# Paced loads, a query-major first group, warm-up matmuls and a reordered end in a grouped-query attention kernel

## The chip, the cores and the metric

The kernel runs on one core of a Trainium2 chip. The metric is the device time of one execution in microseconds. A core has four engines that matter here: PE (matmuls, and weight loads shown as PEld), ACT (activations, here exponentials), DVE (vector operations) and POOL (copies). A fifth, SP, issues all DMAs of this kernel, one after the other in the order of the program. Engines run on their own and are tied by semaphores.

## The reference

Attention with 32 query heads that share 8 key and value heads, batch 16, 288 queries, 512 keys, head size 128, all bfloat16:

```
B, Hq, Hkv, Sq, Sk, D = 16, 32, 8, 288, 512, 128
k = jnp.repeat(k, Hq // Hkv, axis=1)
v = jnp.repeat(v, Hq // Hkv, axis=1)
scores = jnp.einsum("bhqd,bhkd->bhqk", q, k) * D ** -0.5
p = softmax(scores, axis=-1)
out = jnp.einsum("bhqk,bhkd->bhqd", p, v)
```

## The kernel before

**Groups and chunks.** The four query heads of one key head are handled together: 4 x 288 = 1152 query rows, NT = 9 tiles of 128, against 512 keys, NJ = 4 tiles of 128. There are NG = 16 x 8 = 128 such groups. The 4 x 1152 score columns of a group are worked in NC = 3 chunks of CH = 1536 columns, so there are NS = 384 chunks, numbered n. In an ordinary group the columns are key-major: chunk 0 has all 1152 queries of the first key tile and some of the second. The last group (LASTG = 127) is query-major: each chunk has three query tiles against all four key tiles (`pieces`, line 479).

**Steps of a chunk.** `op_s` (line 490, matmul at 499) writes scores S(n) into one of two PSUM buffers ps_s; with two buffers, S(n) waits for the exponential of n - 2. `op_exp` (529, activation at 541) makes the exponential E(n) into pt_sb. The maximum isn't subtracted; at the end the kernel looks at all row sums, and a branch leads to a general path (line 17) if one lies outside a wide range. `op_pv` (509, matmul at 522) makes batch PV(r) of three query tiles from the four key tiles of pt_sb and of the values, with a column of ones added to the values, so that the row sums come out beside the results. It waits for all three exponentials of its group. DVE then takes the reciprocal of the sums (`op_rc`, 556) and scales the batch into o_sb (`op_ev`, 561), which has NO = 6 groups; a scaling waits until the store of the group six before has landed. PV(r) waits for the scaling of r - 2, because ps_o has two banks.

**Order.** PE's order is a loop (line 630): S(n), then PV(n - LAG), LAG = 4. POOL copies each group's values beside the ones (`op_vc`, 544). ACT runs the exponentials in order.

**SP's order.** Queries and keys are loaded with transposing DMAs (`op_q` 448, `op_k` 425), values with plain ones (`op_v` 437). The list `first` (601) loads keys, queries and values of groups 0 to 3 one by one. After it SP branches to its main part and issues a list sorted by a written-out index, in chunks (605 to 617): units of four groups of keys and values (three slots, NSLOT), one q load per group (twelve slots, NQ), one store per group. An index only sets the order; an item also waits for what it needs: a load for its slot, a store for its group's scalings. Loads whose slot has never been used have negative indices, and so stand at the front.

**The end.** The last batch, PV(383), goes to a score buffer instead of ps_o. DVE takes its three reciprocals at once and scales two tiles; ACT scales the third (`op_ev_last`, 574). DVE then looks at the last sums (`op_over`, 590), PE adds the counts over partitions (637), DVE writes a flag (682), every engine loads it and branches. The last group is stored in three parts (472).

Of the kernel before, what the change touches and what calls it, by code (L numbers as in the profile page):

```python
# [6 lines left out]
ACTF = mybir.ActivationFunctionType  # L7
AX = mybir.AxisListType
BF16 = mybir.dt.bfloat16
# [278 lines left out]
def bass_standalone__gqa_softmax__near_ridge_kernel(  # L288
# [6 lines left out]
    B, Hq, Sq, D = q.shape  # L295
    _, Hkv, Sk, _ = k.shape
    P = 128
# [17 lines left out]
    NSLOT = 3  # L315
    NQ = 12
    NPT = 3
    NO = 6
    NS = NG * NC
    LASTG = NG - 1  # L320
# [8 lines left out]
    with ExitStack() as es:  # L329
# [7 lines left out]
        flag_i = es.enter_context(nc.sbuf_tensor("flag_i", [1, 1], I32))  # L337
        block = es.enter_context(nc.Block())

        for name in ["s_go", "s_one", "s_s", "s_e", "s_pv", "s_rc", "s_ev", "s_stat", "s_bad", "s_flag", "s_vc", "s_ol", "s_ea"]:  # L340
            S(name)
        for i in range(NSLOT):
            S("us_k%d" % i)
# [5 lines left out]
            S("s_q%d" % i)  # L349
        for i in range(NO):  # L350
            S("s_o%d" % i)


        gen = ExitStack()
# [4 lines left out]
        def general(eng, key, after):  # L359

            home[key] = nc.cur_bb
            eng.br(after + key)
            with nc.body("general_" + key):
                if key == "sp":
                    eng.sem_inc(sem["s_go"], 1)
                fns[key](eng)
                eng.br("done_" + key)
            nc.switch_bb(after + key)
# [27 lines left out]
        ck_sb = main.enter_context(nc.sbuf_tensor("ck_sb", [P, 3], FP32))  # L396
        bad_sb = main.enter_context(nc.sbuf_tensor("bad_sb", [P, 2, ALONE + 1], FP32))
        one_f = main.enter_context(nc.sbuf_tensor("one_f", [P, 1], FP32))
        dum = main.enter_context(nc.sbuf_tensor("dum", [P, 2], FP32))
        ps_s = main.enter_context(nc.psum_tensor("ps_s", [P, 2, CH], FP32))  # L400
        ps_o = main.enter_context(nc.psum_tensor("ps_o", [P, 2, BANK], FP32))
# [46 lines left out]
        def op_q(g):  # L448
# [3 lines left out]
                    eng.wait_ge(s, n)  # L452
            eng.dma_start_transpose(qt_sb[:, g % NQ], q_v[g * P:(g + 1) * P]).then_inc(sem["s_q%d" % (g % NQ)], 16)  # L453

        def have(kind, g):

            u = g // UG
            if u == 0:
                return ("s_%s%d" % (kind, g), 16)
            return ("us_%s%d" % (kind, u % NSLOT), 16 * (u // NSLOT + (0 if u % NSLOT == 0 else 1)))  # L460

        def op_store(g, i=None):
            eng = nc.sync
            if i is None:
                for (s, n) in need(eng, [("s_ev", NC * (g + 1))]):
                    eng.wait_ge(s, n)
                eng.dma_start(o_v[g], o_sb[:, g % NO].rearrange("p t d -> p (t d)")).then_inc(sem["s_o%d" % (g % NO)], 16)
            else:
                for (s, n) in need(eng, [("s_ev", NC * g + i + 1)] + ([("s_ea", 1)] if i == NC - 1 else [])):
                    eng.wait_ge(s, n)  # L470
                c0, c1 = i * TPC * D, (i + 1) * TPC * D
                eng.dma_start(o_v[g][:, c0:c1], o_sb[:, g % NO].rearrange("p t d -> p (t d)")[:, c0:c1]
                              ).then_inc(sem["s_ol"], 16)
# [4 lines left out]

        def pieces(g, i):

            if g == LASTG:
                w = TPC * P
                cuts = sorted(set(range(0, CH + 1, BANK)) | set(range(0, CH + 1, w)))
                return [(a, a // w, i * w + a % w, b - a) for a, b in zip(cuts[:-1], cuts[1:])]
            lo, hi = i * CH, (i + 1) * CH
            cuts = sorted({lo, hi} | {x for x in range(0, COLS, BANK) if lo < x < hi}
                          | {x for x in range(0, COLS, R) if lo < x < hi})
            return [(a - lo, a // R, a % R, b - a) for a, b in zip(cuts[:-1], cuts[1:])]

        def op_s(n):  # L490
            eng = nc.tensor
            g, i = n // NC, n % NC
            sl, gi = (g // UG) % NSLOT, g % UG
            waits = [have("k", g), ("s_q%d" % (g % NQ), 16 * (g // NQ + 1))]
            if n >= 2:
                waits.append(("s_e", n - 1))
            qg = qt_sb[:, g % NQ].rearrange("d t p -> d (t p)")
            for x, (c, j, r0, w) in enumerate(pieces(g, i)):
                ins = emit(eng, waits if x == 0 else [], lambda: eng.matmul(  # L499
                    ps_s[:, n % 2, c:c + w], kt_sb[:, sl, j, gi, :], qg[:, r0:r0 + w], start=True, stop=True))  # L500
            ins.then_inc(sem["s_s"], 1)
# [7 lines left out]
        def op_pv(r):  # L509
            eng = nc.tensor  # L510
            g = r // NC
            sl, gi = (g // UG) % NSLOT, g % UG
            waits = [("s_vc", g + 1), ("s_e", r + 1 if g == LASTG else NC * (g + 1))]
            if 2 <= r < NS - 1:
                waits.append(("s_ev", r - 1))


            alone = r == NS - 1
            for j in range(NJ):
                for a in range(TPC):  # L520
                    t = TPC * (r % NC) + a
                    ins = emit(eng, waits if a == 0 and j == 0 else [], lambda: eng.matmul(  # L522
                        outs(r)[:, a, :], pt_sb[:, g % NPT, j * R + t * P:j * R + (t + 1) * P],
                        v_sb[:, sl, gi * NJ + j, :], start=(j == 0 and (a == 0 or alone)), stop=(j == NJ - 1),
                        skip_group_check=True))
            ins.then_inc(sem["s_pv"], 1)


        def op_exp(n):
# [2 lines left out]
            waits = [("s_s", n + 1)]  # L532
            if g >= NPT:
                waits.insert(0, ("s_pv", NC * (g - NPT + 1)))
            if g == LASTG:
                w = TPC * P
                dst = pt_sb[:, g % NPT].rearrange("p (j r) -> p j r", r=R)[:, :, i * w:(i + 1) * w]
                src = ps_s[:, n % 2].rearrange("p (j r) -> p j r", r=w)
            else:
                dst, src = pt_sb[:, g % NPT, i * CH:(i + 1) * CH], ps_s[:, n % 2]  # L540
            emit(eng, waits, lambda: eng.activation(dst, src, ACTF.Exp, scale=scale)).then_inc(sem["s_e"], 1)  # L541


        def op_vc(g):
# [16 lines left out]
        def op_ev(r):  # L561
# [3 lines left out]
            if g >= NO:  # L565
                waits.insert(0, ("s_o%d" % (g % NO), 16 * (g // NO)))
            t0 = TPC * (r % NC)
            n = TPC if r < NS - 1 else TPC - 1
            emit(eng, waits, lambda: eng.tensor_tensor(  # L569
                out=o_sb[:, g % NO, t0:t0 + n, :], in0=outs(r)[:, 0:n, 0:D],  # L570
                in1=rl_sb[:, TPC * r:TPC * r + n].unsqueeze(2).broadcast_to([P, n, D]),
                op=ALU.mult)).then_inc(sem["s_ev"], 1)

        def op_ev_last():

            eng = nc.scalar
            emit(eng, [("s_o%d" % (LASTG % NO), 16 * (LASTG // NO)), ("s_rc", NS)], lambda: eng.activation(  # L577
                o_sb[:, LASTG % NO, NT - 1, :], outs(NS - 1)[:, TPC - 1, 0:D], ACTF.Copy,
                scale=rl_sb[:, TPC * NS - 1:TPC * NS])).then_inc(sem["s_ea"], 1)


        def op_stat(b):
# [15 lines left out]
                op0=ALU.is_lt, op1=ALU.add)).then_inc(sem["s_bad"], 1)  # L598


        first = [lambda: op_k(0, 0), lambda: op_q(0), lambda: op_k(0, 1), lambda: op_q(1), lambda: op_v(0, 0)]
        first += [lambda: op_k(0, 2), lambda: op_q(2), lambda: op_v(0, 1)]
        first += [lambda: op_k(0, 3), lambda: op_q(3), lambda: op_v(0, 2), lambda: op_v(0, 3)]

        sp = []
        for u in range(1, NU):
            t = NC * UG * (u - NSLOT + 1) if u >= NSLOT else -2 * NC * UG + u
            sp.append((t + 0.5, lambda u=u: op_k(u)))
            sp.append((t + (LAG if u >= NSLOT else 0.65), lambda u=u: op_v(u)))
        for g in range(UG, NG):  # L610
            t = NC * (g - NQ + 1) + 1.2 if g >= NQ else -2 * NC * UG + g // UG + 0.51 + 0.1 * (g % UG)
            sp.append((t, lambda g=g: op_q(g)))
        for g in range(LASTG):
            sp.append((NC * (g + 1) + LAG + 1.5, lambda g=g: op_store(g)))
# [12 lines left out]

        @block.tensor
        def _(eng):
            for n in range(NS + LAG):  # L630
                if n == NS - 3:
                    hints["pe"] = eng.mark_branch_hint_location()
                if n < NS:
                    op_s(n)
                if n >= LAG:
                    op_pv(n - LAG)
            emit(eng, [("s_ev", NS - 1), ("s_bad", 2)], lambda: eng.matmul(  # L637
                ps_o[0:1, NS % 2, 0:ALONE + 1], one_f[:], bad_sb[:, 1, :], start=True, stop=True)
            ).then_inc(sem["s_bad"], 1)
# [1 line left out]

        @block.scalar
        def _(eng):
            emit(eng, [("s_one", 1)], lambda: eng.activation(dum[:, 1:2], dum[:, 0:1], ACTF.Exp))  # L644
            general(eng, "act", "main_")
            for n in range(NS):
                op_exp(n)
            op_ev_last()
            choose(eng, "act")

        @block.gpsimd
# [6 lines left out]

        @block.vector
        def _(eng):  # L660
            eng.memset(dum[:], 0.0).then_inc(sem["s_one"], 1)  # L661
            eng.memset(one_f[:], 1.0)
            general(eng, "dve", "main_")
            per_b = G * NC
            w0 = NS - 1 - ALONE // TPC
            last = rl_sb[:, NG * NT - ALONE:NG * NT]
            for r in range(NS):
                op_rc(r)
                op_ev(r)
                if r % per_b == per_b - 1 and r < NS - 1:  # L670
# [6 lines left out]
                    eng.tensor_reduce(ck_sb[:, 1:2], st_sb[:, 1, :], AX.X, ALU.min).then_inc(sem["s_stat"], 1)  # L677
                if r == w0 + 2:
                    op_over(ck_sb[:, 0:1], ck_sb[:, 1:2], ALONE, ALONE + 1, ("s_stat", B + 1), B + 2)
            op_over(last, last, 0, ALONE, ("s_rc", NS), B + 3)  # L680
            with nc.allow_low_precision(reason="a count of at most 2048"):
                emit(eng, [("s_bad", 3)], lambda: eng.tensor_reduce(  # L682
                    flag_i[:], ps_o[0:1, NS % 2, 0:ALONE + 1], AX.X, ALU.add)).then_inc(sem["s_flag"], 1)
# [31 lines left out]
```

## Time and profile before

| what | value |
|---|---|
| median of 9 runs | 537.61 us (536.15 to 538.9) |
| profiled execution | 537.46 us |
| its span, first to last instruction | 535.7 us |
| PE busy | 520.0 us, 97% |
| ACT busy | 518.1 us, 97% |
| DVE busy | 288.3 us, 54% |
| POOL busy | 73.7 us, 14% |
| first matmul / first exponential of scores starts at | 6.86 / 8.36 us |
| mean of a 1536-column exponential | 1722 ns |
| mean of a scaling of 128 x 384 | 558 ns |
| PE's granted clock, mean | 0.997 |

The profile is of one execution. Busy times of neighbouring instructions can overlap, so the mean duration of an exponential is longer than the distance from one to the next. "PE ps_s L499" is the score matmul at line 499, "PE ps_o L522" the PV matmul. SPq stands for SP's instructions that issue DMAs; their duration is issue time, and a transfer lands some us after its issue began. "PEld" are weight loads. A chain of waits follows the work that ended last back from step to step.

### The profile page before, as it was taken

The page shows a single profiled execution, that of the slowest core. Times are in us where ns is not written, and L with a number is a line of the kernel's source. Part 1 is how long each engine was busy: PE and PEld are TensorE (multiplying, and loading weights), DVE is VectorE, ACT ScalarE, POOL GpSimd, SP SyncE. Part 2 cuts the span into 40 slices and gives each one's busy share as a digit, 9 for nine tenths or more (in the row PEclk, how much of TensorE's full clock was granted, in tenths as well). Part 3 has the DMA queues.
Part 4 walks back from the last instruction along what each step waited for, and adds up shares of the span by engine and source line. Part 5 has one row for each costly group of instructions (what it writes and reads, how often), then busy time and mean ns, then how long its engine had stood idle before and what let it go on. Part 6 is the DMA issues. An engine that isn't in the chain of part 4 may idle for free.

```text
span 535.7 us, 14538 instructions
## 1 busy us (share of the span) xinstructions
PE 520.0 (97%) x6152; PEld 405.5 (76%) x6152; DVE 288.3 (54%) x809; ACT 518.1 (97%) x387; POOL 73.7 (14%) x133
## 2 busy tenths in 40 slices
PE   4996999999999999999999999999999999999997
PEld 1775777777777777777777777777777777777776
DVE  0543555555555555555555555555555555555555
ACT  4995999999999999999999999999999999999996
POOL 1210111111111100111110111101111101111000
PEclk9998999999999999999999999999999999999999
DMA  7999999999999998989998999999999998985212
GB/s 135 211 198 205 240 237 239 257 218 251 234 262 232 218 213 200 194 224 226 226 220 174 221 210 213 235 199 226 196 214 225 211 220 222 188 216 159 91 67 91
DMA packets 253943, 110.07 MB, mean 205 GB/s; under 512 B 220848, under 2 KB 237616, under 8 KB 253872
## 3 DMA queue, kind: packets, MB, share of 16 engines
q1 hardware_dynamic: 253872, 109.08, 94.7%
q8 instruction: 50, 0.82, 0.7%
q14 instruction: 21, 0.17, 0.1%
HBM read 16.78 MB, written 37.75 MB: 102 GB/s over the span
## 4 chain that ended last, share of the span: by engine, by line
PE 96%; DMA 2%; ACT 1%; DVE 1%; SPq 0%; issue 0%; DVEq 0%
PE ps_o L522 49%; PE ps_s L499 47%; DMA out_dram<-o_sb 1%; DMA qt_sb<-in_q_dram 1%; ACT pt_sb L541 1%; DVE o_sb L569 0%; SPq L432 0%; SPq L453 0%; DVE rl_sb L558 0%; PE ps_o L637 0%; DVE bad_sb L596 0%; DVE flag_i L682 0%; DVE bad_sb L593 0%; DVEq L418 0%
## 5 line engine op out<-in xcount | busy, mean ns | idle before, releaser
L541 ACT ACTIVATE pt_sb<-ps_s 128x1536 bf16<-128x1536 f32 x384 | 516.2, 1722 | 11.8 <-PE ps_s L499 11.8
L522 PEld LDWEIGHTS ps_o<-v_sb,pt_sb 128*128 128x128 bf16 x4596 | 295.6, 98 | 59.6 <-DVE o_sb L569 5.1
L522 PE MATMUL ps_o<-v_sb,pt_sb 128*128 128x129 bf16 x4596 | 327.1, 221 | 4.7 <-DVE o_sb L569 4.7
L499 PE MATMUL ps_s<-qt_sb,kt_sb 128*128 128x512 bf16 (+3 forms) x1542 | 316.3, 328 | 7.8 <-DMA qt_sb<-in_q_dram 6.9
L569 DVE TENSOR_TENSOR o_sb<-ps_o,rl_sb 128x384 bf16<-128x384 f32 x383 | 213.6, 558 | 19.1 <-DMA out_dram<-o_sb 5.6
L558 DVE RECIPROCAL rl_sb<-ps_o 128x3 f32<-128x3 f32 x383 | 69.3, 181 | 225.1 <-PE ps_o L522 225.1
L499 PEld LDWEIGHTS ps_s<-qt_sb,kt_sb 128*128 128x128 bf16 x1542 | 117.3, 98 | 67.1 <-DMA qt_sb<-in_q_dram 6.9
L551 POOL COPY v_sb<-vd_sb 128x512 bf16<-128x512 bf16 x128 | 73.2, 616 | 416.9 <-DMA vd_sb<-in_v_dram 353.2
L588 DVE TENSOR_REDUCE st_sb<-rl_sb 128x1 f32<-128x72 f32 (+1 forms) x16 | 3.5, 217 | 0.0
L586 DVE TENSOR_REDUCE st_sb<-rl_sb 128x1 f32<-128x72 f32 (+1 forms) x16 | 3.5, 217 | 0.0
L577 ACT ACTIVATE o_sb<-ps_s,rl_sb 128x128 bf16<-128x128 f32 x1 | 0.4, 367 | 2.2 <-DVE rl_sb L558 2.2
L644 ACT ACT_TABLE_LOAD x1 | 1.3, 1283 | 0.8 <-PEq L700 0.8
L637 PE MATMUL ps_o<-bad_sb,one_f 128*1 128x25 f32 x2 | 0.2, 184 | 1.0 <-DVE bad_sb L596 1.0
L637 PEld LDWEIGHTS ps_o<-bad_sb,one_f 128*1 128x1 f32 x2 | 0.1, 80 | 1.2 <-DVE bad_sb L596 1.2
L522 PE MATMUL ps_s<-v_sb,pt_sb 128*128 128x129 bf16 x12 | 0.9, 220 | 0.0
L522 PEld LDWEIGHTS ps_s<-v_sb,pt_sb 128*128 128x128 bf16 x12 | 0.7, 98 | 0.0
L661 DVE MEMSET dum<- 128x2 f32 x1 | 0.1, 60 | 0.9 <-PEq L700 0.9
L569 DVE TENSOR_TENSOR o_sb<-ps_s,rl_sb 128x256 bf16<-128x256 f32 x1 | 0.4, 425 | 0.0
L653 POOL MEMSET v_sb<- 128x48 bf16 x1 | 0.3, 311 | 0.3 <-POOLq L700 0.3
L682 DVE TENSOR_REDUCE flag_i<-ps_o 1x1 int32<-1x25 f32 x1 | 0.2, 170 | 0.3 <-PE ps_o L637 0.3
L644 ACT ACTIVATE dum<-dum 128x1 f32<-128x1 f32 x1 | 0.2, 202 | 0.0
L596 DVE SCALAR_TENSOR_TENSOR bad_sb<-rl_sb,bad_sb 128x24 f32<-128x24 f32 x1 | 0.2, 184 | 0.0
(11 smaller groups left out, 1.4 us busy)
## 6 DMA issues: line engine op xcount, KB each, us to landing
out_dram<-o_sb SPq DMA_DIRECT2D x127, 288.0 KB, 3.5
vd_sb<-in_v_dram SPq DMA_DIRECT2D x31, 512.0 KB, 5.2
qt_sb<-in_q_dram SPq DMA_TRANSPOSE x128, 4.8
kt_sb<-in_k_dram SPq DMA_TRANSPOSE x35, 5.0
vd_sb<-in_v_dram SPq DMA_DIRECT2D x4, 128.0 KB, 3.1
out_dram<-o_sb SPq DMA_DIRECT2D x3, 96.0 KB, 1.6
```

What stands on the lines that cost most here:

```text
L499: ins = emit(eng, waits if x == 0 else [], lambda: eng.matmul(ps_s[:, n % 2, c:c + w], kt_sb[:, sl, j, gi, :], qg[:, r0:r0 + w], start=Tru ...
L522: ins = emit(eng, waits if a == 0 and j == 0 else [], lambda: eng.matmul(outs(r)[:, a, :], pt_sb[:, g % NPT, j * R + t * P:j * R + (t + 1) ...
L541: emit(eng, waits, lambda: eng.activation(dst, src, ACTF.Exp, scale=scale)).then_inc(sem["s_e"], 1)
L551: emit(eng, waits, lambda: eng.tensor_copy(v_sb[:, sl, gi * NJ:(gi + 1) * NJ, 0:D], vd_sb[:, sl, gi].rearrange("p (j d) -> p j d", d=D))). ...
L558: emit(eng, [("s_pv", r + 1)], lambda: eng.reciprocal(rl_sb[:, TPC * r:TPC * (r + 1)].unsqueeze(2), outs(r)[:, :, D:DV])).then_inc(sem["s_ ...
L569: emit(eng, waits, lambda: eng.tensor_tensor(out=o_sb[:, g % NO, t0:t0 + n, :], in0=outs(r)[:, 0:n, 0:D], in1=rl_sb[:, TPC * r:TPC * r + n ...
L577: emit(eng, [("s_o%d" % (LASTG % NO), 16 * (LASTG // NO)), ("s_rc", NS)], lambda: eng.activation(o_sb[:, LASTG % NO, NT - 1, :], outs(NS - ...
L586: emit(eng, [("s_rc", e // TPC)], lambda: eng.tensor_reduce(st_sb[:, 0, b:b + 1], rl_sb[:, a:e], AX.X, ALU.max))
L588: eng.tensor_reduce(st_sb[:, 1, b:b + 1], rl_sb[:, a:e], AX.X, ALU.min).then_inc(sem["s_stat"], 1)
L637: emit(eng, [("s_ev", NS - 1), ("s_bad", 2)], lambda: eng.matmul(ps_o[0:1, NS % 2, 0:ALONE + 1], one_f[:], bad_sb[:, 1, :], start=True, st ...
L644: emit(eng, [("s_one", 1)], lambda: eng.activation(dum[:, 1:2], dum[:, 0:1], ACTF.Exp))
L653: eng.memset(v_sb[:, :, :, D:DV], 1.0)
```

## The change

Seven things are changed. The index of an item in SP's sorted list is now bounded from below by 1/1.4 of the time of its use, for loads into fresh slots too, and a unit's values follow its keys at once in the first two units. Group 0 is query-major, as the last one is; its q load is cut into three DMAs of three tiles each, with a semaphore for each, and S(0), S(1) and S(2) each wait for their own. Eight 512-column matmuls of zeros run on PE into ps_o before S(0); DVE zeroes their operand. ACT's branch to its main part carries a hint. Near the end PV(379) comes ahead of S(383) in PE's order instead of behind it. The last exponential is issued in two parts, for two query tiles and for one. PV(383) is worked tile by tile, and its tiles get two reciprocals (two tiles, then one) and are scaled one by one, the first and third on DVE, the second on ACT.

```diff
+    WARM = 8
...
         def general(eng, key, after):
...
-            eng.br(after + key)
+            br = eng.br(after + key)
+            if key in hints:
+                br.branch_hint(hints[key])
...
+        def op_q0(i):
+            c0, c1 = i * TPC, (i + 1) * TPC
+            nc.sync.dma_start_transpose(qt_sb[:, 0, c0:c1], q_v[0:P, c0 * D:c1 * D]).then_inc(sem["s_qp%d" % i], 16)
+
+        def have_q(g, i):
+            if g == 0:
+                return ("s_qp%d" % i, 16)
+            return ("s_q%d" % (g % NQ), 16 * (g // NQ + (0 if g % NQ == 0 else 1)))
...
-                for (s, n) in need(eng, [("s_ev", NC * g + i + 1)] + ([("s_ea", 1)] if i == NC - 1 else [])):
+                for (s, n) in need(eng, [("s_ev", NC * g + i + 1)] if i < NC - 1 else [("s_ea", 1), ("s_ev", NS + 1)]):
...
-            if g == LASTG:
+            if g in (0, LASTG):
...
-            waits = [have("k", g), ("s_q%d" % (g % NQ), 16 * (g // NQ + 1))]
+            waits = [have("k", g), have_q(g, i)]
...
+        def op_pv_last(a):
+
+            eng = nc.tensor
+            sl, gi = (LASTG // UG) % NSLOT, LASTG % UG
+            t = NT - TPC + a
+            for j in range(NJ):
+                ins = emit(eng, [("s_e", NS + (0 if a < TPC - 1 else 1))], lambda: eng.matmul(
+                    outs(NS - 1)[:, a, :], pt_sb[:, LASTG % NPT, j * R + t * P:j * R + (t + 1) * P],
+                    v_sb[:, sl, gi * NJ + j, :], start=(j == 0), stop=(j == NJ - 1)))
+            if a > 0:
+                ins.then_inc(sem["s_pv"], 1)
...
-            emit(eng, waits, lambda: eng.activation(dst, src, ACTF.Exp, scale=scale)).then_inc(sem["s_e"], 1)
+            parts = [(dst, src)]
+            if n == NS - 1:
+                w -= P
+                parts = [(dst[:, :, 0:w], src[:, :, 0:w]), (dst[:, :, w:w + P], src[:, :, w:w + P])]
+            for (d, s) in parts:
+                emit(eng, waits, lambda: eng.activation(d, s, ACTF.Exp, scale=scale)).then_inc(sem["s_e"], 1)
...
+        def op_rc_last(a0, a1):
+            eng = nc.vector
+            c = TPC * (NS - 1)
+            emit(eng, [("s_pv", NS + (0 if a1 < TPC else 1))], lambda: eng.reciprocal(
+                rl_sb[:, c + a0:c + a1].unsqueeze(2), outs(NS - 1)[:, a0:a1, D:DV])).then_inc(sem["s_rc"], 1)
+
+        def op_ev_last(a):
+
+            c, t = TPC * (NS - 1) + a, NT - TPC + a
+            waits = [("s_o%d" % (LASTG % NO), 16 * (LASTG // NO)), ("s_rc", NS + (0 if a < TPC - 1 else 1))]
+            dst, src, by = o_sb[:, LASTG % NO, t, :], outs(NS - 1)[:, a, 0:D], rl_sb[:, c:c + 1]
+            if a == 1:
+                emit(nc.scalar, waits, lambda: nc.scalar.activation(dst, src, ACTF.Copy, scale=by)).then_inc(sem["s_ea"], 1)
+            else:
+                emit(nc.vector, waits, lambda: nc.vector.tensor_scalar(
+                    out=dst, in0=src, scalar1=by, scalar2=None, op0=ALU.mult)).then_inc(sem["s_ev"], 1)
...
-        first = [lambda: op_k(0, 0), lambda: op_q(0), lambda: op_k(0, 1), lambda: op_q(1), lambda: op_v(0, 0)]
+        first = [lambda: op_k(0, 0)] + [lambda i=i: op_q0(i) for i in range(NC)] + [lambda: op_k(0, 1), lambda: op_q(1), lambda: op_v(0, 0)]
...
-            t = NC * UG * (u - NSLOT + 1) if u >= NSLOT else -2 * NC * UG + u
-            sp.append((t + 0.5, lambda u=u: op_k(u)))
-            sp.append((t + (LAG if u >= NSLOT else 0.65), lambda u=u: op_v(u)))
+            t = max(NC * UG * (u - NSLOT + 1) + 0.5, NC * (UG * u - 2.5) / 1.4 - 0.2)
+            sp.append((t, lambda u=u: op_k(u)))
+            sp.append((t + (LAG if u >= NSLOT else 0.15), lambda u=u: op_v(u)))
         for g in range(UG, NG):
-            t = NC * (g - NQ + 1) + 1.2 if g >= NQ else -2 * NC * UG + g // UG + 0.51 + 0.1 * (g % UG)
+            t = max(NC * (g - NQ + 1) + 1.2, NC * (g - 2.5) / 1.4)
             sp.append((t, lambda g=g: op_q(g)))
...
         def _(eng):
-            for n in range(NS + LAG):
+            for x in range(WARM):
+                emit(eng, [("s_z", 1)], lambda: eng.matmul(
+                    ps_o[:, 1, :], z_sb[:, 0:P], z_sb[:], start=True, stop=True))
+            r = 0
+            for n in range(NS):
                 if n == NS - 3:
                     hints["pe"] = eng.mark_branch_hint_location()
-                if n < NS:
-                    op_s(n)
-                if n >= LAG:
-                    op_pv(n - LAG)
+                op_s(n)
+                while r <= n - LAG + (1 if n >= NS - 2 else 0):
+                    op_pv(r)
+                    r += 1
+            while r < NS - 1:
+                op_pv(r)
+                r += 1
+            for a in range(TPC):
+                op_pv_last(a)
...
+            hints["act"] = eng.mark_branch_hint_location()
             emit(eng, [("s_one", 1)], lambda: eng.activation(dum[:, 1:2], dum[:, 0:1], ACTF.Exp))
             general(eng, "act", "main_")
             for n in range(NS):
                 op_exp(n)
-            op_ev_last()
+            op_ev_last(1)
...
+            eng.memset(z_sb[:], 0.0).then_inc(sem["s_z"], 1)
             eng.memset(dum[:], 0.0).then_inc(sem["s_one"], 1)
...
-            for r in range(NS):
+            for r in range(NS - 1):
                 op_rc(r)
                 op_ev(r)
...
-            op_over(last, last, 0, ALONE, ("s_rc", NS), B + 3)
+            op_rc_last(0, TPC - 1)
+            op_ev_last(0)
+            op_rc_last(TPC - 1, TPC)
+            op_ev_last(TPC - 1)
+            op_over(last, last, 0, ALONE, ("s_rc", NS + 1), B + 3)
```

More of the change, by code (lines that the diff above doesn't have):

```diff
@@ L338, in bass_standalone__gqa_softmax__near_ridge_kernel @@
         block = es.enter_context(nc.Block())
-        for name in ["s_go", "s_one", "s_s", "s_e", "s_pv", "s_rc", "s_ev", "s_stat", "s_bad", "s_flag", "s_vc", "s_ol", "s_ea"]:
+        for name in ["s_go", "s_one", "s_s", "s_e", "s_pv", "s_rc", "s_ev", "s_stat", "s_bad", "s_flag", "s_vc", "s_ol", "s_ea", "s_z"]:
             S(name)
@@ L351, in bass_standalone__gqa_softmax__near_ridge_kernel @@
             S("s_o%d" % i)
+        for i in range(NC):
+            S("s_qp%d" % i)
         gen = ExitStack()
@@ L398, in bass_standalone__gqa_softmax__near_ridge_kernel @@
         one_f = main.enter_context(nc.sbuf_tensor("one_f", [P, 1], FP32))
+        z_sb = main.enter_context(nc.sbuf_tensor("z_sb", [P, BANK], BF16))
         dum = main.enter_context(nc.sbuf_tensor("dum", [P, 2], FP32))
@@ L515, in op_pv @@
                 waits.append(("s_ev", r - 1))
-            alone = r == NS - 1
             for j in range(NJ):
@@ L523, in op_pv @@
                         outs(r)[:, a, :], pt_sb[:, g % NPT, j * R + t * P:j * R + (t + 1) * P],
-                        v_sb[:, sl, gi * NJ + j, :], start=(j == 0 and (a == 0 or alone)), stop=(j == NJ - 1),
+                        v_sb[:, sl, gi * NJ + j, :], start=(j == 0 and a == 0), stop=(j == NJ - 1),
                         skip_group_check=True))
             ins.then_inc(sem["s_pv"], 1)
+        def op_pv_last(a):
[8 more added lines that the diff above has]
+                ins.then_inc(sem["s_pv"], 1)
         def op_exp(n):
@@ L534, in op_exp @@
                 waits.insert(0, ("s_pv", NC * (g - NPT + 1)))
-            if g == LASTG:
+            if g in (0, LASTG):
                 w = TPC * P
@@ L567, in op_ev @@
             t0 = TPC * (r % NC)
-            n = TPC if r < NS - 1 else TPC - 1
             emit(eng, waits, lambda: eng.tensor_tensor(
-                out=o_sb[:, g % NO, t0:t0 + n, :], in0=outs(r)[:, 0:n, 0:D],
-                in1=rl_sb[:, TPC * r:TPC * r + n].unsqueeze(2).broadcast_to([P, n, D]),
+                out=o_sb[:, g % NO, t0:t0 + TPC, :], in0=outs(r)[:, :, 0:D],
+                in1=rl_sb[:, TPC * r:TPC * (r + 1)].unsqueeze(2).broadcast_to([P, TPC, D]),
                 op=ALU.mult)).then_inc(sem["s_ev"], 1)
[L574 to L579, printed above, removed]
+        def op_rc_last(a0, a1):
[12 more added lines that the diff above has]
+                    out=dst, in0=src, scalar1=by, scalar2=None, op0=ALU.mult)).then_inc(sem["s_ev"], 1)
         def op_stat(b):
```

## The prediction

> **What bounds the kernel now.** I read the waits first, because every engine that matters is above 95% busy and shares say nothing then. Columns: who waited for what, total us, times, longest.
>
> ```profile
> DVE o_sb L569 <- DMA out_dram<-o_sb: 5.6, 1, 5.6
> PEld ps_o L522 <- DVE o_sb L569: 5.1, 2, 4.8
> ACT pt_sb L541 <- PE ps_s L499: 11.8, 3, 6.1
> ```
>
> Two holes only: ACT stands 6.1 us until the first scores, and once in the middle a scaling on DVE waits 5.6 us for a store, PE behind it, ACT behind PE. The chain of waits around the second hole (start us, us, what):
>
> ```profile
> 37.62 1.21 SPq L453
> 38.83 0.04 issue
> 38.88 5.19 DMA out_dram<-o_sb
> 44.07 0.03 issue
> ...
> 44.17 0.57 DVE o_sb L569
> 44.74 0.05 issue
> 44.78 1.48 PE ps_o L522 x12
> 46.26 1.28 PE ps_s L499 x4
> 47.54 1.07 PE ps_o L522 x12
> 48.61 0.65 PE ps_s L499 x4
> ```
>
> The store of group 0 is issued only at 38.88, because SP first works off all loads up to q13. It lands at 44.07, and the scaling of batch 18 (group 6, which reuses the six-deep o_sb) waits for it. Three PE batches then take 1.48, 1.28 and 1.07 us where 0.69, 0.65 and 0.69 are usual.
>
> The timeline of SP (start us, us) says what each early load costs to issue:
>
> ```profile
> 2.18 1.35 SPq L453 DMA_TRANSPOSE qt_sb<-in_q_dram  x1
> 3.58 1.26 SPq L432 DMA_TRANSPOSE kt_sb<-in_k_dram  x1
> 4.88 1.41 SPq L453 DMA_TRANSPOSE qt_sb<-in_q_dram  x1
> ...
> 12.83 1.06 SPq L444 DMA_DIRECT2D vd_sb<-in_v_dram  x2
> 14.42 2.49 SPq L432 DMA_TRANSPOSE kt_sb<-in_k_dram  x1
> 16.95 2.90 SPq L453 DMA_TRANSPOSE qt_sb<-in_q_dram  x2
> 19.90 0.58 SPq L444 DMA_DIRECT2D vd_sb<-in_v_dram  x1
> 20.53 4.08 SPq L453 DMA_TRANSPOSE qt_sb<-in_q_dram  x2
> ```
>
> SP stands still for only 2.3 us of the first 45: there its own issue time, and not the memory alone, sets when a load starts. Everywhere else one slot (one S, one PV, one exponential) repeats every 1.338 to 1.344 us; exponentials started at 8.36, 9.71, 11.10, 12.45 and 13.78 while PE had slack, so ACT alone needs about 1.345 and PE 0.65 + 0.69 = 1.34. Both are full. A delay of either is not made up.
>
> [...] after 4.5 idle us the batches above took twice as long for about 3 us. [...] here everything is on SP, and that issue time is what counts. [...] the trace shows 0.53 us on SP between 13.89 and 14.42, and none on ACT's path, whose branch at 2.3 us lies 6 us before its first exponential.
>
> **The change, part by part.**
>
> Paced loads. SP's list after the first loads becomes K1, V1, q4, q5, q6, store 0, q7, store 1, K2, V2 and so on (index 3.01, 3.16, 3.21, 5.36, 7.5, 8.5, 9.64, 11.5, 11.59, 11.74 from the new formulas; K1 is the unit of groups 4 to 7). Store 0 stands behind 5 loads instead of 14. By the durations above it goes out near 25 us and lands by 31; batch 18 needs it at about 40. Stores 1 to 6 by the same sum go out at 28, 35, 37, 43, 46 and 49 and are wanted from 42 on, every 4 us; none is late. The hole goes. Its size: S12 starts at 23.36 in the timeline and S26 at 48.45; 14 slots of 1.342 would end at 42.15, so 6.3 us come back (4.5 idle and 1.8 at half clock).
>
> Query-major group 0. Its q load is cut in three, so S0 needs only the first piece. SP's issue: 9 tiles of 128 cost 1.31 to 1.41, 4 tiles (one K) 1.20 to 1.32; the slope is about 0.03 a tile, so a piece of 3 tiles costs about 1.17 (low end 0.6, as a plain load; high end 2.5, as the K unit). Three pieces with two gaps of 0.05 instead of 1.35 put all that follows on SP off by 3 x 1.17 + 0.10 - 1.35 = 2.26 us. First piece: issued 2.18, landing after 3.0 to 4.6 (the first K and the first q), say 3.6, at 5.8. S0 warm takes 0.82, so the first exponential starts near 6.7 instead of 8.36. But q1 is now issued at 4.88 + 2.26 = 7.14 and lands 3.6 later (as before) at 10.7; S3 ends at 11.4, E3 starts at 11.5. Before it was 12.45. Of 1.7 us, 0.9 is left. V0 is copied by 12.3, when PV0 wants it; q2 lands at 14.1 for S6 at 14.3, q3 at 17.3 for S9 at 18.4: covered.
>
> Where the stall goes. K1 is issued at 14.42 + 2.26 = 16.68, takes 2.49; V1 has moved ahead of q4 (before, q4 and q5 went first) at 19.21 with 0.58; so q4 is issued at 19.84 instead of 16.95. A q right behind V1 landed after 5.1 in the trace (the one at 20.53), others nearby after 4.4 to 6.1. So q4 lands at 24.9 (24.2 to 25.9), and S12 starts at 25.0: its earlier pace wants it at 22.4, and it was 23.36 before. The 0.9 is gone and 1.6 more. q5 (21.5, lands 26.5, wanted 29) and later loads have margin, growing with each group. PE idles 2.5 us there, [...] so I leave the clock warm; if it goes cold, add 1.8 as in the old hole.
>
> PE warm. Zeroing 128 x 512 on DVE (not shown; 0.06 for two columns, at most 0.7 by the scalings' 558 and 425 ns drawn out to 512 columns) precedes the dummy exponential's operand, hidden by the 1.28 us table load. Eight 512-column matmuls at half clock, about 0.43 each (from 1.48 for 1536 columns), end near 4.7, before the piece lands. Worth at most 0.66 of S0 (1.48 to 0.82), and that lies in the 0.9 that q4 takes back. ACT's branch hint: nothing, under 6 us of cover; without it at most the 0.53 seen on SP.
>
> The end. The last lines of before, chain of waits:
>
> ```profile
> 529.45 0.57 DVE o_sb L569
> 530.02 0.05 issue
> 530.07 0.88 PE ps_o L522 x12
> ```
>
> PV379 now precedes S383; so E383 starts 0.6 us later, in two parts, and PV381 no longer waits for DVE (PE idled 0.18, PEld 0.35). But PV382 wants the scaling of PV380, which starts after S383 as before (529.05), and is free at 530.70: PV382 starts at 530.75, as it did. E383's second part ends near 531.0, before PV383's third tile at 531.9: hidden by 0.9. Then tile order: a=1 ends 0.23 us earlier than the whole, the first reciprocal at 532.1, the first scaling 532.33. A 128-column scaling from PSUM isn't shown; 384 columns take 558 ns and 256 take 425, so 292 [...]. Reciprocal of the third at 532.54, scaling 532.75 to 533.04, check at 532.96 against 532.90: +0.06 (bounds -0.2 to +0.3). The last store goes out with it.
>
> Sum: S26 at 25.0 + 14 x 1.342 = 43.8 against 48.45, -4.7; end +0.06; together -4.6. Span 535.7 - 4.6 = 531.1; with the 1.76 us around it (537.46 - 535.7) 532.9. The profiled time stands 0.15 under the median of 537.61, which is inside the runs' spread, so I leave 532.9.
>
> **Rivals.**
> Full gain: q4 isn't late, because pieces are issued at 0.6 each (0.5 us later in all instead of 2.26) or q4 lands after 3.6 as the first ones did. Then S12 starts between 22.4 and 23.4: -7.2 to -6.2, 530.3 to 531.3. For it: landings of 3.5 to 3.7 before 14 us. Against: every landing between 15 and 31 us took 4.4 or more, with the DMA share at or above 1.
> Cold after the new hole, or q4 after 8 us (the longest of the trace): +1.8 to +3.1, 534.7 to 536. [...]
> Slower: a piece reads a third of each row, and its issue might cost as much as the K unit or more. The new hole eats the old one's 6.3 when S12 starts at 29.7; that is 4.7 later than forecast, so at 1.17 + 4.7/3 = 2.7 us a piece or above, less with a cold clock; at 3.2 us the time is about 539. For it: the K unit's 2.49 with four times the rows of one K. Against: one K with fewer rows and narrow source costs 1.2.
> The pacing misses: another store is late, and a hole of 4 us or more comes back, 537. Against: over 7 us margin by the sum above.
>
> **From cases to numbers.** New hole at S12 0.60 (532 to 534), full gain 0.22, cold or late 0.09, slower 0.06, pacing misses 0.03. 0.2% is 1.1 us, about what can be told here. Faster 0.90 (the first three, less a little), same 0.04, slower 0.06. The range 530.4 to 535.0 takes in the first two and the lower part of the third.
>
> **What would show it.** Right: no wait of DVE L569 for a store; a wait of PE's S for a q load of 2 to 3 us near 22 to 25; three q pieces of about 1.2 us each on SP; first exponential near 6.7; the fourth behind a wait for q1; the last PV in the same place relative to the last S. Wrong: no wait near 22 us (then about 531), half-clock batches after it (then 535 or more), pieces above 2 us, or a new wait for out_dram.

## The result and the profile after

| what | before | after |
|---|---|---|
| median | 537.87 us (31 runs) | 534.37 us (10 runs) |
| span of the profiled execution | 535.7 us | 532.6 us |
| S12 starts | 23.36 us | 25.99 us |
| S382's start to the end of the span | 9.35 us | 9.60 us |

The ratio of the runs, which is not the quotient of the two medians, is 0.9942, 95% interval 0.993 to 0.9954: 0.6% faster. The forecast was 532.9 us in a range of 530.4 to 535.0; of the 4.6 us that it expected in the span, 3.1 came.

The waits of the changed kernel (who waited for what: total us, times, longest):

```profile
DVE o_sb L599 <- DMA out_dram<-o_sb: 0.4, 1, 0.4
PE ps_s L514 <- DMA qt_sb<-in_q_dram: 5.8, 5, 2.8
ACT pt_sb L572 <- PE ps_s L514: 7.9, 4, 3.5
```

The wait for a store has shrunk from 5.6 to 0.4 us. In before PE waited for queries only once, 6.9 us at the start; now it waits five times, and ACT four times for PE. The chain of waits in the first 28 us (start us, us, what) says which of these decided:

```profile
13.99 1.36 SPq L459
...
16.98 1.88 SPq L438
...
19.54 6.32 DMA qt_sb<-in_q_dram
...
25.99 0.81 PE ps_s L514 x4
26.80 0.69 PE ps_o L536 x12
```

It runs along SP's issues, through the load of q4 (19.54 to 25.86), to S12. The first exponential, 2.5 us earlier than before (5.85), isn't on this chain at all. (The chain ties q4's landing to its issue; the run without warm-up below shows the limit of that.) The timeline of SP (start us, us) has the loads in the order that the prediction wrote down, with store 0 out at 26.30 instead of 38.88:

```profile
2.18 3.93 SPq L463 DMA_TRANSPOSE qt_sb<-in_q_dram  x3
...
16.98 1.88 SPq L438 DMA_TRANSPOSE kt_sb<-in_k_dram  x1
18.91 0.58 SPq L450 DMA_DIRECT2D vd_sb<-in_v_dram  x1
19.54 6.72 SPq L459 DMA_TRANSPOSE qt_sb<-in_q_dram  x3
26.30 0.58 SPq L482 DMA_DIRECT2D out_dram<-o_sb  x1
```

The end, in the timeline of DVE (start us, us):

```profile
528.53 0.56 DVE L599 TENSOR_TENSOR o_sb<-ps_o,rl_sb 128x384 bf16<-128x384 f32 x1
529.00 0.16 DVE L607 RECIPROCAL rl_sb<-ps_s 128x2 f32<-128x2 f32 x1
529.20 0.35 DVE L618 TENSOR_SCALAR o_sb<-ps_s,rl_sb 128x128 bf16<-128x128 f32 x1
529.46 0.16 DVE L607 RECIPROCAL rl_sb<-ps_s 128x1 f32<-128x1 f32 x1
529.66 0.35 DVE L618 TENSOR_SCALAR o_sb<-ps_s,rl_sb 128x128 bf16<-128x128 f32 x1
529.93 0.17 DVE L633 TENSOR_SCALAR bad_sb<-rl_sb 128x24 f32<-128x24 f32 x1
```

DVE is still scaling batch 382 when the first two tiles of 383 are there, so the tile-by-tile order finds it busy. Counted from S382's start, the look at the sums (L633) begins at 6.93 us; in before it began at 6.55.

### The profile page after: what moved, and what is told of

It is laid out like the page before. It is cut to its first block, busy times and chain, and to the rows that moved or that the text cites. A ratio compares the mean times of both kernels' runs of the same rounds, so it can differ in the third digit from the quotient of the medians.

```text
span 532.6 us, 14574 instructions
## 1 busy us (share of the span) xinstructions
PE 522.0 (98%) x6166; PEld 406.2 (76%) x6166; DVE 288.9 (54%) x812; ACT 518.7 (97%) x388; POOL 73.9 (14%) x133
## 4 chain that ended last, share of the span: by engine, by line
PE 94%; SPq 3%; DMA 1%; DVE 1%; issue 0%
PE ps_o L536 48%; PE ps_s L514 46%; SPq L438 1%; DMA qt_sb<-in_q_dram 1%; SPq L459 1%; SPq L463 1%; SPq L450 1%; DVE o_sb L599 0%; DVE o_sb L618 0%; DVE rl_sb L589 0%; PE ps_o L686 0%; DVE bad_sb L636 0%; DVE rl_sb L607 0%; DVE flag_i L737 0%; DVE bad_sb L633 0%
## 5 line engine op out<-in xcount | busy, mean ns | idle before, releaser
L671 PE MATMUL ps_o<-z_sb 128*128 128x512 bf16 x8 | 3.4, 604 | 1.3 <-DVE z_sb L711 1.3
```

Of the source, the lines that this page charges most:

```text
L671: emit(eng, [("s_z", 1)], lambda: eng.matmul(ps_o[:, 1, :], z_sb[:, 0:P], z_sb[:], start=True, stop=True))
```

## The experiments

The theory after the profile: the pacing gives back the hole (6.3 us); the query-major start takes more than 2 us of it, because its two extra transposing DMAs set SP back and q4, behind V1, is late; warm-up and end give nothing or cost a little. The main rivals: V1's new place, not the pieces, makes q4 late; or the earlier first exponential is a gain of its own.

**Pacing alone.** Before, with the new indices only.

```diff
-            t = NC * UG * (u - NSLOT + 1) if u >= NSLOT else -2 * NC * UG + u
-            sp.append((t + 0.5, lambda u=u: op_k(u)))
-            sp.append((t + (LAG if u >= NSLOT else 0.65), lambda u=u: op_v(u)))
+            t = max(NC * UG * (u - NSLOT + 1) + 0.5, NC * (UG * u - 2.5) / 1.4 - 0.2)
+            sp.append((t, lambda u=u: op_k(u)))
+            sp.append((t + (LAG if u >= NSLOT else 0.15), lambda u=u: op_v(u)))
...
+            t = max(NC * (g - NQ + 1) + 1.2, NC * (g - 2.5) / 1.4)
```

> The kernel before with the new indices of SP's list alone. My theory: the pacing removes the hole of 6.3 us at batch 18, and without the three q pieces SP is 2.5 us earlier than in the changed kernel, so q4 is issued near 17.3 and lands near 23.5 (6.2 later, as with V1 ahead of it in the changed kernel); S12, wanted at 23.36, waits at most 0.6. Time 5.7 to 6.3 us under before, about 532.0: faster than the whole change. Rival A (the new wait comes from V1 standing ahead of q4, not from the pieces): the wait at S12 stays 1.5 us or more, time about 534. Rival B (the query-major start is a gain of its own): the time is above that of the whole change, 535 or more.

Measured: 532.02 us against 537.15 of before on the same chip; ratio 0.9919 (0.9888 to 0.9949), span 530.1. ACT in its timeline, after the start:

```profile
11.38 49.81 ACT L541 ACTIVATE pt_sb<-ps_s 128x1536 bf16<-128x1536 f32 x37 [0.21 <-PE ps_s L499]
```

From 11.38 on ACT has no hole: 37 exponentials in one stretch across the place where batch 18 stood before. Here q4 was issued at 17.46 and landed after 6.2, at 23.6, so S12 started at 23.76, 0.1 us after the PV ahead of it was done. Pacing alone is faster than the whole change. By how much isn't sharp: the spans differ by 2.5 us (530.1 and 532.6) and the medians by 2.4, but the medians come from different chips, on which those of before differ by 0.7; the two ratios differ by 1.2 us, and their intervals overlap at the edges. Rivals A and B both fall: V1 ahead of q4 does lengthen the landing (6.2 us here, 5.3 in before), but by itself it makes no long stall, because without the pieces q4 is issued 2.1 us earlier.

**The start alone.** Before, with group 0 query-major and its q load in three; the waits for the pieces are those of the change.

```diff
+        def op_q0(i):
+            c0, c1 = i * TPC, (i + 1) * TPC
+            nc.sync.dma_start_transpose(qt_sb[:, 0, c0:c1], q_v[0:P, c0 * D:c1 * D]).then_inc(sem["s_qp%d" % i], 16)
...
-            if g == LASTG:
+            if g in (0, LASTG):
...
-        first = [lambda: op_k(0, 0), lambda: op_q(0), lambda: op_k(0, 1), lambda: op_q(1), lambda: op_v(0, 0)]
+        first = [lambda: op_k(0, 0)] + [lambda i=i: op_q0(i) for i in range(NC)] + [lambda: op_k(0, 1), lambda: op_q(1), lambda: op_v(0, 0)]
```

> The kernel before with group 0 query-major and its q load in three pieces, nothing else. My theory: the first exponential starts near 6.7 (no warm-up), but everything behind on SP is 2.5 us later: store 0 goes out near 41.4, lands near 46.6, the hole ends 2.5 us later than in before. Time about 540.2, slower. Rival (the earlier first exponential is kept): 0.9 to 2.5 us faster than before, 535.5 to 537.

Measured: 540.25 us, ratio 1.0062 (1.004 to 1.0083): slower. A wait and two lines of SP's timeline:

```profile
DVE o_sb L580 <- DMA out_dram<-o_sb: 6.9, 1, 6.9
```

```profile
17.10 1.68 SPq L434 DMA_TRANSPOSE kt_sb<-in_k_dram  x1
...
43.01 0.58 SPq L478 DMA_DIRECT2D out_dram<-o_sb  x1
```

K1 goes out 2.7 us later than in before (14.42), store 0 4.1 us later (38.88), it lands 2.3 us later (46.4), and the wait for it is 1.3 us longer. The first exponential began at 6.83 instead of 8.36, and nothing of that was left. With more on SP than it can issue in time, an earlier first step is paid for later.

**The end alone.** Before, with PV379 ahead of S383, the last exponential in two parts and the last batch tile by tile, as in the change's diff; none of the rest.

> The kernel before with only the changes at the end (PV379 ahead of S383, last exponential in two parts, PV383 tile by tile, its scalings one by one). My theory, after the profile of the whole change: PV382 starts 4.41 us after S382 as before, because it waits for the scaling of PV380; DVE is busy with the scaling of 382 when the first two tiles are ready, so the reciprocals start no earlier, and two reciprocals and two scalings take 0.38 us more than one and one. The span from S382's start to the end grows from 9.35 to 9.6 or 9.7; the time is 0.3 us longer, within what can be told. Rival (the tile order pays): the span from S382 to the end falls by 0.2 or more.

Measured: 537.46 against 537.15 us, ratio 1.0 (0.998 to 1.002): no difference in time. In its profile S382 starts at 526.56 and the span ends at 536.2, 9.64 us later, against 9.35 in before. The rival, a gain of 0.2 us or more, doesn't show.

**V1 behind q5.** The whole change, with one number altered.

```diff
-            sp.append((t + (LAG if u >= NSLOT else 0.15), lambda u=u: op_v(u)))
+            sp.append((t + (LAG if u >= NSLOT else 2.5), lambda u=u: op_v(u)))
```

> The whole change, but the values V1 (and V2) stand 2.5 in the index behind their keys instead of 0.15, so V1 comes after q5. My theory: V1's 512 KB share the DMA engines with K1 and q4; without them q4 is issued at 18.9 instead of 19.5 and lands after 5.3 instead of 6.3, near 24.2. S12 starts 1.6 us earlier, time 532.7. Rival (only the issue order on SP counts): 0.6 us earlier, 533.8. Rival (K1, not q4, is the late one): no change, 534.4.

Measured: 532.11 us, ratio 0.9919 (0.9887 to 0.995), span 530.4: 2.2 us of span for one number. SP's timeline from K1 on, ACT's from the fourth exponential on, and then the landing of the q load issued at 18.63:

```profile
16.88 1.71 SPq L438 DMA_TRANSPOSE kt_sb<-in_k_dram  x1
18.63 4.21 SPq L459 DMA_TRANSPOSE qt_sb<-in_q_dram  x2
22.89 0.58 SPq L450 DMA_DIRECT2D vd_sb<-in_v_dram  x1
```

```profile
12.51 48.83 ACT L572 ACTIVATE pt_sb<-ps_s 128x1536 bf16<-128x1536 f32 x36 [2.12 <-PE ps_s L514]
```

```profile
DMA to landing us min/median/max: 5.4/5.4/5.4
```

q4 goes out 0.9 us earlier than in the change and lands after 5.4 instead of 6.3 us, at 24.0. ACT's hole at S12 (1.6 us in the change) is gone: S12 starts at 24.12, 1.9 us earlier. That is more than the rival's 0.6 for the issue order alone. How the 1.9 us divide between the earlier issue and the missing 512 KB of V1 between K1 and q4 isn't shown by this run; the next one speaks against the issue.

**No warm-up.** The whole change without the eight matmuls and the zeroing.

```diff
-            for x in range(WARM):
-                emit(eng, [("s_z", 1)], lambda: eng.matmul(
-                    ps_o[:, 1, :], z_sb[:, 0:P], z_sb[:], start=True, stop=True))
...
-            eng.memset(z_sb[:], 0.0).then_inc(sem["s_z"], 1)
```

> The whole change without the eight matmuls of zeros and the zeroing. My theory: S0 runs at half clock and the first exponential starts 0.5 to 0.7 us later, but S3 still waits for q1 and S12 for q4, whose times SP sets; S12 starts at 26.0 as in the whole change. Time 534.4, no difference. Rival (the warm clock is needed at the start): 0.5 us or more later, 535 or above.

Measured: 533.8 us, ratio 0.9942 (0.9926 to 0.9958), the same ratio as the whole change. S0 took 1.46 us instead of 0.83 and the first exponential started at 6.55 instead of 5.85, yet E12 started at 26.75 (26.84 with warm-up). The load decides, not the clock.

The run also says more about that load. V1's issue took 2.24 us here instead of 0.58 (why was not looked for), so q4 went out 1.39 us later than in the change:

```profile
18.64 2.24 SPq L450 DMA_DIRECT2D vd_sb<-in_v_dram  x1
20.93 5.18 SPq L459 DMA_TRANSPOSE qt_sb<-in_q_dram  x3
...
25.90 0.81 PE L514 MATMUL ps_s<-qt_sb,kt_sb 128*128 128x512 bf16 x4 [1.80 <-DMA qt_sb<-in_q_dram]
```

Yet it landed after 4.8 us instead of 6.3, at 25.76, 0.1 us earlier than in the change. So at this place the moment of q4's issue doesn't set its landing. What the two runs share is K1 and V1 in flight ahead of q4: they landed at 22.89 and 24.62 here, at 23.41 and 24.91 in the change. The DMA engines are nearly full as well: in the profile of before the packets of this queue take 94.7% of the time of all 16.

**The old end.** The whole change with the end of before, and without ACT's branch hint.

> The whole change with the end of before (and without the branch hint on ACT). My theory: S382's start to the end takes 9.35 us again instead of 9.6, all else stays; time 534.1, 0.3 under the whole change, not to be told apart by times but by the profile. Rival (the new end hides something that the old one shows once the hole is gone): 0.3 us or more longer than the whole change.

Measured: 533.4 us, ratio 0.994 (0.9926 to 0.9954), not to be told from the whole change. By the profile S382 starts at 522.28 and the span ends at 531.6: 9.32 us, as in before. With the run of the end alone, the end is seen from both sides: it costs 0.3 us. ACT's first exponential came at 5.93 without the hint, 5.85 with it; no wait there shows what the hint could have saved.

**Pacing with V1 behind.** The kernel before with the paced indices and 2.5 in place of 0.15; nothing else.

> The kernel before with the paced indices and V1 behind q5, nothing else (whole q load of group 0). My theory: q4 lands near 22.3, S12 doesn't wait (wanted 23.36); the first exponential at 8.4 and ACT's pace set everything: 0.2 to 0.5 us under the run with pacing alone, about 531.7. Rival (another load is late once V1 is behind): a new wait, 532.5 or more.

Measured: 531.56 us, ratio 0.9909 (0.9886 to 0.9932), span 529.7. ACT's timeline:

```profile
8.39 52.50 ACT L541 ACTIVATE pt_sb<-ps_s 128x1536 bf16<-128x1536 f32 x39 [6.09 <-PE ps_s L499]
```

One stretch from the first exponential on. What is left is the start itself. With this run there are four cases for S12. It started at 23.33 with neither the pieces nor V1 ahead of q4, at 23.76 with V1 ahead alone, at 24.12 with the pieces (and the rest of the change) but V1 behind, and at 25.99 with both; the runs without warm-up and with the old end, which have both, gave 25.90 and 25.57. The long stall takes the pieces and V1's new place together.

**Fewer issues at the start.** The whole change with the old end and V1 behind, q of group 0 in two pieces, and keys and values of groups 1 to 3 in one DMA each. The first pair of lines stands in `op_k` and in `op_v` alike.

```diff
-            g0, g1 = (0, UG) if gi is None else (gi, gi + 1)
+            g0, g1 = (0, UG) if gi is None else ((0, 1) if gi == 0 else (1, UG))
...
-            c0, c1 = i * TPC, (i + 1) * TPC
+            c0, c1 = (0, TPC) if i == 0 else (TPC, NT)
...
+        first = [lambda: op_k(0, 0), lambda: op_q0(0), lambda: op_q0(1), lambda: op_k(0, 1), lambda: op_q(1), lambda: op_v(0, 0)]
+        first += [lambda: op_q(2), lambda: op_v(0, 1), lambda: op_q(3)]
```

> The whole change with the old end, and with SP freed at the start: q of group 0 in two pieces (3 tiles, 6 tiles), keys of groups 1 to 3 in one DMA, values of groups 1 to 3 in one DMA, V1 and V2 behind the q loads as in the run with V1 behind. My theory: five issues fewer; q1 lands near 10.2 and q4 near 21, both no later than the exponentials want them but for about 1 us at q1. The fourth exponential starts near 10.9 and nothing waits for a load after that. Time 530.2. Rival (the larger key load lands late and S3 waits for it): fourth exponential at 12 or later, 531.5 or above.

Measured: 530.69 us, ratio 0.9898 (0.9867 to 0.9929), span 528.7: the fastest of all, below before and the change. ACT's timeline:

```profile
6.32 1.45 ACT L554 ACTIVATE pt_sb<-ps_s 128x1536 bf16<-128x1536 f32 x1 [4.02 <-PE ps_s L512]
8.38 2.79 ACT L554 ACTIVATE pt_sb<-ps_s 128x1536 bf16<-128x1536 f32 x2 [0.60 <-PE ps_s L512]
11.38 49.81 ACT L554 ACTIVATE pt_sb<-ps_s 128x1536 bf16<-128x1536 f32 x37 [0.22 <-PE ps_s L512]
```

The fourth exponential starts at 11.38, 0.5 us later than expected, because S1 waited for the six-tile piece (0.60 us on ACT, second line) and S3 for q1 (0.22 us). It is 1 us ahead of the run with pacing and V1 behind, where the fourth exponential came at about 8.39 + 3 x 1.345 = 12.4, and the spans differ by 1.0. So the query-major start, with the warm-up, does pay once SP has room for it. What each of these two gives was not separated. That fewer issues alone would give nothing is argued, not shown: without the pieces ACT already had no hole after its first exponential. The two ratios' intervals overlap, but both runs are from one chip, and six of the seven times here (530.40 to 530.78) lie below the lowest there (531.19).

## Why the prediction was right, and where it was off

**The hole at batch 18 goes: right.** The wait for a store fell from 5.6 to 0.4 us (and the 0.4 is another store, at 117.9 us), store 0 went out at 26.3 (forecast near 25), store 1 at 28.3 (28). Pacing alone took 5.6 us off the span, of the 6.3 forecast; 0.4 of the rest is S12, which started at 23.76 there and at 23.36 in before: 0.1 of it is the wait for q4, the other 0.3 came with S2 and S3, which took 2.80 us together there and 2.17 in before.

**The stall moves to q4 at S12: right in place and in its two causes, too small by 1.0 us.** Issue went as worked out: pieces 1.24 to 1.35 each (forecast 1.17), K1 at 16.98 (16.68), q4 at 19.54 (19.84, as K1's issue took 1.88 and not 2.49). The failed term is "a q right behind V1 landed after 5.1": it landed after 6.32, and S12 started at 25.99 instead of 25.0. The range given there, 24.2 to 25.9, just held it. The analogy was wrong in one thing: the load that gave 5.1 had V1 ahead of it, but K1 had landed by then; in the change K1, V1 and q4 are in flight together, and K1 itself took 6.4 instead of 5.0. The form of the term, issue plus a fixed landing time, is also in doubt: q4 landed after 5.4 with V1 behind and after 4.8 without warm-up, where it was issued 1.39 us later and landed at the same time. Why K1 lands later behind the pieces (5.6 to 6.4 us in every run that has three, 4.5 to 5.1 in those with a whole load) stays open.

**The first exponential, near 6.7: too late.** It started at 5.85, because the first piece landed after 2.8 us instead of 3.6.

**0.9 us left at the fourth exponential: wrong, at no cost here.** It started at 12.80 (forecast 11.5, before 12.45). q1 landed at 11.2, 0.5 later than forecast, and S3 and S4 ran at half clock (2.72 us for both), of which the forecast had nothing: PE's idle time was considered for S12, not for S3. E12 waited for q4 in any case, as the run without warm-up shows again.

**The clock stays warm at S12: right, but in part by luck.** S12 took 0.81 us. The forecast was a pause of 2.5 us. That such a pause leaves the clock up was the author's assumption; before shows one fall in its span, at 44.80, after 4.49 idle us, and no pause near 2.5. Because the fourth exponential was late, PE idled only 1.57 us at S12. At S3 a pause of 2.82 us, and of 2.13 with V1 behind, did end at half clock, so the forecast pause was not tested.

**The end, +0.06: too small.** The runs with only the end and with only the old end give +0.3. PV382 did wait for the scaling of 380 and started 4.41 us after S382 in both kernels, as forecast. What failed is "the first reciprocal at 532.1": it missed that the scaling of 382 keeps DVE until 0.25 us after that. Also, a 128-column scaling took 350 ns, not 292.

**The sum.** Forecast -4.6; q4 +1.0, end +0.2 in this profile, and 0.3 that is spread over the 370 slots between S12 and S382 (497.0 us, 1.3433 a slot, where 1.342 was used for the first 14 and the sequence of before for the rest) give -3.1, the change of the span. The last 0.3 is not shown to come from the change: with V1 behind, without warm-up and with the old end the same stretch took 496.7 us each time. Its cause was not followed up.

**Two readings in the working.** "ACT alone needs about 1.345" is too much: in before the exponentials E3 to E24 started from 12.45 to 40.38, 1.330 apart, while S5 to S12 came every 1.344. PE sets the slot, and ACT has a little room. And 0.43 us for a matmul of zeros doesn't follow from the 1.48 that it names (a third of it is 0.49); a third of the score batch's 1.28 gives it, and the eight did take 3.40. The forecast hung on neither.

## What to carry to other kernels

When one queue issues all loads, write out its schedule with issue times before cutting a load into pieces: each transposing DMA cost 1.2 to 1.5 us of the queue at the start, for 3 tiles as for 12, and what was gained at the first step came back as a late load a dozen steps on. Write down too what is in flight ahead of each load: from K1 on, q4's landing did not follow its issue. A load that isn't needed yet should not be issued between two that are. To free buffers, stores must not stand behind loads that nobody waits for.

## What was not expected of the hardware

Ahead of the first load of a whole unit, the issue time of a transposing DMA hardly depended on its size: 1.24 to 1.44 us for 3 tiles of 128 x 128, 1.19 to 1.32 for 4, 1.31 to 1.54 for 9, and 1.48 for the 12 tiles of the three groups' keys in one DMA.

PE's granted clock fell to half in pauses at the start about as long as the 2.5 us over which the prediction left it up, or shorter. In the change the last matmul of S2 ended at 8.51 and S3 started at 11.32; the clock was at half from 11.16, 2.65 us after the end of S2, to 14.57. The table of stages, with the granted clock third from the right:

```profile
12.00:13.00 1.00, 1.00 (x5) 0.41 (x4) 0.00 (x0) 0.20 (x1) 0.61 (x1) 0.50 0.70 116
```

With V1 behind, the last matmul ended at 8.90 and the clock fell at 10.82, only 1.9 us later (mean granted clock of the first 26 us: 0.93, as in the change). A pause of 1.80 us after dense use, before S12 in the run without warm-up, left it at full (S12 took 0.81 us). The stretches at half clock lasted 3.41 us in the change, with V1 behind and in before (44.80 to 48.22), and twice that, 6.83, in the run with the start alone (mean granted clock 0.994, where before has 0.997).

Nor was PE idle all through the 3.41 us before the fall: it was busy for 0.8 us of them in the change and with V1 behind, and for 0.6 with the old end. How long a pause takes the clock down, or how much use keeps it up, isn't shown.

The granted clock that the table gives for before isn't to be read ahead of its first change, at 44.80: it says 1.00 for the first matmuls, S0 and S1, though they took 2.74 us together; S3 and S4 took 1.51 in the run with fewer issues.
